# All last output transfers through SP, and a new order of the whole kernel

## The chip, the cores and the metric

One core of a Trainium2 chip (trn2). The metric is the time of one execution on the device in microseconds (us), as the median of several runs; less is better. The engines are TensorE (PE), VectorE (DVE), ScalarE (ACT), GpSimd (POOL) and SyncE (SP, here a queue that does nothing but issue DMA transfers).

## What is computed

```python
def _attn_ref(q, k, v):            # q, k, v: (4, 8, 576, 64) float32
    # 1: means over 4 neighbouring positions, full softmax attention, each row repeated 4 times
    out_up = np.repeat(sm_attn(q_d, k_d, v_d), 4, axis=2)
    # 2: softmax attention on the full sequence, |i - j| < 4 only
    out_local = np.matmul(attn, v)
    return out_up + out_local

x = attn_out.transpose(0, 2, 1, 3).reshape(B * S, H * D)   # 2304 x 512
h = (x @ w1) * (x @ w2) @ w3                               # d_ff 1024
x = h @ w_out
h = np.maximum(np.maximum(x @ w1, x @ w2), x @ w3)         # second layer, d_ff 768
out = h @ w_out                                            # 2304 x 512
```

## The kernel before, in words

The sequence of each of the 4 batches is cut into slabs. `down` (L503) does the attention on the means for one batch and one pair of heads: it loads `qk` and four `vp` planes (the first through SP, the other three through POOL, which adds them up, L515). `slab` (L604) does the attention on the band for one slab: it loads the rows of v (tile `vw`, printed as `area`) through SP in many small transfers (L629 by way of `dma`, L424); PE makes the scores (`sq`, L643); DVE and ACT the softmax (L651 to L663); PE turns it (`ptq`, L669) and multiplies by v (`poq`, L688); DVE adds the part on the means (`x32`, L697), and ACT and DVE split the sum into a high and a low part (`xt`, L449 and L451). All large products are made of three matmuls of such parts (`mm3`, L456 to L458).

Weights arrive as 64-bit words (`raw`, through SP) and are made float32 by one ACT and four DVE instructions (`float32`, L476 to L482, tiles `wf` and `cv`). While the attention of the first slabs runs, PE also makes the product of w3 and w_out (`weights_product`, `pw`, L750). When three slabs are there and the first weights, the products of the first layer begin (`front`, `pf`, L456 to L458, and `back`, `py`), and behind them those of the second (`pb`). From the first `pf` to the last `pb` the matmuls of the two layers follow one another.

Results are copied by ACT (L996) or DVE (L998) into output tiles by `put` (L985 to L1009). The tokens are done in groups `rd`; `NR - 1` is the last. Of four output rows of a group two go out singly through `dma` (L424, 128x384, 192 KB) and two as a pair (L1003, 128x2x384, 384 KB). In the last group the pairs are issued by POOL, everywhere else by SP.

The order of the work is a table: `ORDER` (L69) holds for each engine the numbers of its tasks, 2567 in all, one after another. `Program.order` merges the five lists into one program with a model of the time (`AFTER`, `RATE`, `COME`, L251 to L257); where a tile may take one of several places, the merge also says which. An engine's own instructions follow its list. SP's transfers use eight semaphores in turn, so a transfer's issue waits for the landing of the one eight ahead of it (`DMAHW0` to `DMAHW7` in the orders below).

Of the kernel before, what the change touches and what calls it, by code (L numbers as in the profile page):

```python
# [16 lines left out]
P = 128  # L17
# [117 lines left out]
    "ACT":  # L135
# [52 lines left out]
}  # L188
LAG = 1

SHORT = 2.2

WARM = 8
EARLY = 5
MM = 0.175


def view(ap, offset, dims):

# [48 lines left out]
class Program:  # L248


    AFTER = {"PE": 0.16, "DVE": 0.12, "ACT": 0.15, "POOL": 0.15, "SP": 2.3}  # L251
    RATE = 0.33e6
    ADDS, MORE = 2.2, 4.5

# [1086 lines left out]
```

## Time and profile before

| | us |
|---|---|
| median of 3 runs | 756.31 (755.21 to 756.64) |
| the profiled execution, its own time | 753.49 |
| its span in the trace | 751.7 |
| PE busy | 728.7 |
| DVE, ACT, POOL busy | 508.4, 338.7, 52.8 |
| TensorE clock, mean share of full speed | 0.990 |

The profiled execution is 2.82 us below the median of the runs, and 1.79 us above its span. PE is busy for 97% of the span, so a look at the rest, some 23 us, and at where PE ran at a low clock, tells what there is to win without less work for PE. Waits of the other engines count only where PE, or the end, waits for them.

### The profile page before, as it was taken

The page shows a single profiled execution, that of the slowest core. Times are in us where ns is not written, and L with a number is a line of the kernel's source. Part 1 is how long each engine was busy: PE and PEld are TensorE (multiplying, and loading weights), DVE is VectorE, ACT ScalarE, POOL GpSimd, SP SyncE. Part 2 cuts the span into 40 slices and gives each one's busy share as a digit, 9 for nine tenths or more (in the row PEclk, how much of TensorE's full clock was granted, in tenths as well). Part 3 has the DMA queues.
Part 4 walks back from the last instruction along what each step waited for, and adds up shares of the span by engine and source line. Part 5 has one row for each costly group of instructions (what it writes and reads, how often), then busy time and mean ns, then how long its engine had stood idle before and what let it go on. Part 6 is the DMA issues. An engine that isn't in the chain of part 4 may idle for free.

```text
span 751.7 us, 16174 instructions
## 1 busy us (share of the span) xinstructions
PE 728.7 (97%) x6636; PEld 580.8 (77%) x6636; DVE 508.4 (68%) x866; ACT 338.7 (45%) x737; POOL 52.8 (7%) x117
## 2 busy tenths in 40 slices
PE   7898999999999999999999999999999999999994
PEld 3444467777777778777888899888888888889994
DVE  6996899767334452444385789888766775488883
ACT  6672577546643673322343365532222221134683
POOL 2400401003010210000000000000000000000001
PEclk9998999999999999999999999999999999999997
DMA  9889755124332322021485696678675666786306
GB/s 335 254 246 267 180 185 143 46 66 88 94 68 66 71 65 67 14 52 36 140 308 195 211 310 227 236 276 274 220 274 196 241 241 231 276 287 225 99 30 223
DMA packets 63337, 132.72 MB, mean 177 GB/s; under 512 B 23360, under 2 KB 42608, under 8 KB 60192
## 3 DMA queue, kind: packets, MB, share of 16 engines
q1 hardware_dynamic: 58320, 126.97, 50.3%
q0 software_dynamic: 4944, 4.72, 3.8%
q8 instruction: 52, 0.85, 0.5%
q14 instruction: 21, 0.17, 0.1%
HBM read 90.28 MB, written 41.39 MB: 175 GB/s over the span
## 4 chain that ended last, share of the span: by engine, by line
PE 90%; DVE 5%; DMA 2%; issue 1%; ACT 0%; POOL 0%; POOLq 0%; SPq 0%; ACTq 0%; DVEq 0%
PE pb L456 12%; PE pb L458 12%; PE pb L457 12%; PE pf L456 9%; PE pf L458 9%; PE pf L457 9%; PE py L456 5%; PE pw L750 5%; PE py L457 4%; PE py L458 4%; PE poq L688 3%; PE sq L643 2%; PE po L589 1%; PE sp L540 1%; DVE wf L480 1%; DVE wf L482 1%
## 5 line engine op out<-in xcount | busy, mean ns | idle before, releaser
L456 PE MATMUL pf<-xt,w 128*128 128x504 f32 (+1 forms) x320 | 121.1, 378 | 0.5 <-DVE x L697 0.5
L456 PE MATMUL pb<-xc,wu 128*128 128x504 f32 (+1 forms) x324 | 120.6, 372 | 0.3
L458 PE MATMUL pb<-xc,wu 128*128 128x504 f32 (+1 forms) x324 | 119.6, 369 | 0.0
L457 PE MATMUL pb<-xc,wu 128*128 128x504 f32 (+1 forms) x324 | 119.6, 369 | 0.0
L458 PE MATMUL pf<-xt,w 128*128 128x504 f32 (+1 forms) x320 | 118.9, 372 | 0.0
L457 PE MATMUL pf<-xt,w 128*128 128x504 f32 (+1 forms) x320 | 118.7, 371 | 0.0
L456 PEld LDWEIGHTS pb<-xc,wu 128*128 128x128 f32 x324 | 60.9, 188 | 13.9 <-DVE t L912 4.1
L456 PEld LDWEIGHTS pf<-xt,w 128*128 128x128 f32 x320 | 60.1, 188 | 12.0 <-ACT dp L582 1.0
L458 PEld LDWEIGHTS pb<-xc,wu 128*128 128x128 f32 x324 | 60.9, 188 | 10.3
L914 ACT COPY t<-pb 128x504 f32<-128x504 f32 x36 | 20.9, 581 | 106.3 <-PE pb L458 93.9
L457 PEld LDWEIGHTS pb<-xc,wu 128*128 128x128 f32 x324 | 60.9, 188 | 9.8
L458 PEld LDWEIGHTS pf<-xt,w 128*128 128x128 f32 x320 | 60.1, 188 | 10.2
L457 PEld LDWEIGHTS pf<-xt,w 128*128 128x128 f32 x320 | 60.3, 188 | 9.7
L912 DVE TENSOR_TENSOR t<-t,pb 128x504 f32<-128x504 f32 x60 | 40.2, 677 | 38.2 <-PE pb L458 21.7
L750 PE MATMUL pw<-wf 128*128 128x512 f32 x128 | 61.3, 624 | 4.8 <-DVE wf L482 4.8
L456 PE MATMUL py<-g,wp 128*128 128x504 f32 (+1 forms) x160 | 63.2, 395 | 0.0
L457 PE MATMUL py<-g,wp 128*128 128x504 f32 (+1 forms) x160 | 59.6, 372 | 0.0
L458 PE MATMUL py<-g,wp 128*128 128x504 f32 (+1 forms) x160 | 59.3, 371 | 0.0
L782 DVE TENSOR_TENSOR z<-pf,z 128x504 f32<-128x504 f32 (+1 forms) x40 | 25.4, 635 | 42.6 <-PE pf L458 39.6
L750 PEld LDWEIGHTS pw<-wf 128*128 128x128 f32 x128 | 24.0, 197 | 32.2 <-issue 25.5
L458 PE MATMUL pb<-go,wm 128*128 128x252 f32 x168 | 46.8, 279 | 0.0
L456 PE MATMUL pb<-go,wm 128*128 128x252 f32 x168 | 46.8, 279 | 0.0
(140 smaller groups left out, 1339.4 us busy)
## 6 DMA issues: line engine op xcount, KB each, us to landing
wu<-w_dram SPq DMA_DIRECT2D x18, 1024.0 KB
w_dram<-hl SPq DMA_DIRECT2D x20, 512.0 KB
qk<-qkp SPq DMA_DIRECT2D x16, 576.0 KB
raw<-m SPq DMA_DIRECT2D x18, 512.0 KB
raw<-w3t SPq DMA_DIRECT2D x16, 512.0 KB
raw<-w SPq DMA_DIRECT2D x16, 512.0 KB
w_dram<-hls SPq DMA_DIRECT2D x16, 512.0 KB
m_dram<-hls SPq DMA_DIRECT2D x12, 512.0 KB
```

Source lines behind the costliest of these rows:

```text
L456: nc.tensor.matmul(o, wlo, xhi, start=first, stop=False, skip_group_check=again)
L457: nc.tensor.matmul(o, whi, xlo, start=False, stop=False, skip_group_check=again)
L458: nc.tensor.matmul(o, whi, xhi, start=False, stop=last, skip_group_check=again)
L480: prog.add(dve(n), lambda e: e.scalar_tensor_tensor(u(), high(), 0xC0000000, u(), op0=ALU.bitwise_and, op1=ALU.bitwise_or), [words], cv)
L482: prog.add(dve(n), lambda e: e.scalar_tensor_tensor(u(), low(), 29, u(), op0=ALU.logical_shift_right, op1=ALU.bitwise_or), [words], cv)
L540: e.matmul(sps[a]()[:KH, half * GD:(half + 1) * GD], s()[h, half * KH:(half + 1) * KH], s()[h, GD:2 * GD], start=True, stop=True,)
L643: e.matmul(sps[a]()[j * 32:(j + 1) * 32, (half * HP + hp) * BK:(half * HP + hp + 1) * BK], q[h, t:t + 32], k[h, t:t + BK], start=True, sto ...
L688: e.matmul(pos[hp]()[a * D:(a + 1) * D, i * BQ:(i + 1) * BQ], vw()[h, a, i], pt().rearrange("p a n -> p (a n)")[h, c:c + BQ], start=True, ...
L750: e.matmul(os[i](), w()[:, i * P:(i + 1) * P], o(), start=n == 0, stop=n == NF - 1)
L782: prog.add(psum(n), lambda e, pp=pp: e.tensor_tensor(z()[:, :n], pp()[:, :n], z()[:, :n], op=ALU.mult), [pp], [z])
L912: prog.add(dve(N), lambda e: e.tensor_tensor(ap(o), ap(x), ap(y), op=op), [x, y], [o])
L914: copy = lambda o, x: prog.add(act(N), lambda e: e.copy(ap(o), ap(x)), [x], [o])
```

## The change

```diff
+ROWS = 1.35
-    AFTER = {"PE": 0.16, "DVE": 0.12, "ACT": 0.15, "POOL": 0.15, "SP": 2.3}
-    RATE = 0.33e6
+    AFTER = {"PE": 0.16, "DVE": 0.12, "ACT": 0.15, "POOL": 0.15, "SP": 2.1}
+    RATE = 0.345e6
-    HAND, COME = 165, 45
+    HAND, COME = 165, 55
...
-                        [], [(vw, (hp, part, offset))], BV // 2 * (4096 if h == slice(0, 2) else 2048 * 7))
+                        [], [(vw, (hp, part, offset))], BV // 2 * (4096 if h == slice(0, 2) else 2048 * 7) * ROWS)
...
-                prog.add(("POOL", 1.0) if rd == NR - 1 else ("SP", 0.43), lambda e, rd=rd, j=j, o=o[0][0]: e.dma_start(
-                    out[rd * NJ + j, KX // 2:].rearrange("l p t -> p l t"), view(o(), 0, [[T, 2], [1, T]])),
-                    [t for t, _ in o], [], size=P * T * 8)
+                dma(lambda rd=rd, j=j: out[rd * NJ + j, KX // 2:].rearrange("l p t -> p l t"),
+                    lambda o=o[0][0]: view(o(), 0, [[T, 2], [1, T]]), [t for t, _ in o], [], P * T * 8)
...
-    "0 1 20 2 3 4 5 315 6 29 7 31 47 316 124 317 33 318 125 58 56 74 319 320 60 83 85 101 321 135 87 322 159 112 "
-    "110 160 114 331 137 332 138 170 194 333 195 334 172 335 173 336 447 205 337 207 338 208 458 456 474 609 611 "
+    "0 1 20 2 3 4 5 6 7 31 29 47 315 316 124 317 318 33 58 56 319 74 320 125 321 60 83 85 101 87 322 135 159 112 "
+    "160 331 110 114 332 137 138 333 170 194 334 195 335 172 336 173 337 447 205 338 207 208 458 456 474 609 611 "
```

The number 1.35 and the three rates are in the model alone: the bytes that are moved and the work that is done stay. The three pairs of the last group go through SP instead of POOL. All five lists of `ORDER` are new; of PE's the first two rows are shown (the second half of PE's list is the same as before). In them 315 to 322 and 331 to 338 are the sixteen steps of the weight product (eight matmuls each on the chip), 137 and 138 the two halves of slab 0's product with v, 205 the turn of the third slab's softmax, 609 the first product of the first layer.

On SP, around the last rows of v for slab 0 (`area<-v0`), before:

```order
L424 DMA raw_569<-w3t 128x1024 [waits DMAHW5_49]
L424 DMA raw_518<-w3t 128x1024 [waits DMAHW6_49]
L424 DMA raw_569<-w3t 128x1024 [waits DMAHW7_49]
L424 DMA area_372<-v0 15x2x512 [waits DMAHW0_49]
L424 DMA area_372<-v0 15x2x512 [waits DMAHW1_49]
L424 DMA area_372<-v0 15x2x512 [waits DMAHW2_49]
L424 DMA raw_619<-w12 128x1024 [waits DMAHW3_49,DVE_49,PE_49]
L424 DMA area_372<-v0 15x2x512 [waits DMAHW4_49]
L424 DMA area_372<-v0 15x2x512 [waits DMAHW5_49]
L424 DMA area_372<-vl 15x8x64 [waits DMAHW6_49]
```

and now (the last `v0` row here is slab 1's, the four others are slab 0's):

```order
L426 DMA area_395<-v0 15x2x512 [waits DMAHW6_49]
L426 DMA raw_447<-w3t 128x1024 [waits DMAHW7_49]
L426 DMA raw_682<-w12 128x1024 [waits DMAHW0_49,DVE_49,Activation_49]
L426 DMA area_395<-v0 15x2x512 [waits DMAHW1_49]
L426 DMA area_395<-v0 15x2x512 [waits DMAHW2_49]
L426 DMA area_395<-v0 15x2x512 [waits DMAHW3_49]
L517 DMA area_171<-vp 72x256 [waits DMAHW4_49,DMASW7_49,PE_49]
L426 DMA area_395<-v0 15x2x512 [waits DMAHW5_49]
L426 DMA raw_682<-w12 128x1024 [waits DMAHW6_49]
```

Five rows of slab 0 stood around the first `w12` load before, behind three `w3t` loads. Now the last three of slab 0 stand behind a `w12` load that waits for DVE to have converted what its buffer held, and the rows of slab 1 begin behind a `vp` load that waits for PE.

On DVE, around the additions behind slab 0's `poq`, before:

```order
L663 TENSOR_TENSOR s_684<-s_684,mx_707 128x512 [waits DVE_49]
L697 TENSOR_TENSOR x32_801<-poq_716,od_389 128x192 [waits PE_49]
L697 TENSOR_TENSOR x32_803<-poq_713,od_389 128x192
L697 TENSOR_TENSOR x32_801<-poq_719,od_389 128x192 [waits PE_49]
L477 TENSOR_SCALAR wf_520<-wf_520 128x1024
L478 TENSOR_SCALAR wf_520<-wf_520 128x1024 [waits DVE_49]
L480 SCALAR_TENSOR_TENSOR wf_520<-raw_569,wf_520 128x1024 [waits DMAHW7_49,DMAHW5_49,DVE_49]
L482 SCALAR_TENSOR_TENSOR wf_520<-raw_569,wf_520 128x1024 [waits DVE_49]
L697 TENSOR_TENSOR x32_803<-poq_710,od_389 128x192
```

and now:

```order
L665 TENSOR_TENSOR s_657<-s_657,mx_684 128x512 [waits DVE_49]
L479 TENSOR_SCALAR wf_653<-wf_653 128x1024
L480 TENSOR_SCALAR wf_653<-wf_653 128x1024 [waits DVE_49]
L482 SCALAR_TENSOR_TENSOR wf_653<-raw_447,wf_653 128x1024 [waits DMAHW7_49,DMAHW4_49,DVE_49]
L699 TENSOR_TENSOR x32_800<-poq_721,od_376 128x192 [waits PE_49]
L699 TENSOR_TENSOR x32_800<-poq_724,od_376 128x192 [waits PE_49]
L699 TENSOR_TENSOR x32_803<-poq_718,od_376 128x192
L484 SCALAR_TENSOR_TENSOR wf_653<-raw_447,wf_653 128x1024 [waits DVE_49]
L699 TENSOR_TENSOR x32_803<-poq_715,od_376 128x192
L479 TENSOR_SCALAR cv_792<-cv_792 128x1024 [waits Activation_49]
```

Three of the four conversion instructions of the last `w3t` part now stand ahead of the first addition that waits for PE. Up to the last `xt` that the first `pf` needs, DVE's list holds three conversions of `cv` (L477 to L482) where it held two; of the rest it holds as many as before.

On SP at the end, now, the nine transfers of the last group (before, the three `128x2x384` of them stood on POOL, as its last three transfers, and the six others on SP):

```order
L426 DMA out<-area_7248 128x2x384 [waits DMAHW1_49,DVE_49,Activation_49]
L426 DMA out<-area_7372 128x384 [waits DMAHW2_49,Activation_49]
L426 DMA out<-area_7372 128x384 [waits DMAHW3_49,DVE_49]
L426 DMA out<-area_7418 128x384 [waits DMAHW4_49]
L426 DMA out<-area_7320 128x2x384 [waits DMAHW5_49,DVE_49,Activation_49]
L426 DMA out<-area_7418 128x384 [waits DMAHW6_49]
L426 DMA out<-area_7701 128x384 [waits DMAHW7_49]
L426 DMA out<-area_7701 128x384 [waits DMAHW0_49,Activation_49]
L426 DMA out<-area_7248 128x2x384 [waits DMAHW1_49,Activation_49]
```

The last pair now waits for the landing of the first one, which is eight ahead of it.

## Rows read from the trace of the kernel before

**Rows 1.** The page: busy time of PE, its share of the span, instructions.
```profile
PE 728.7 (97%) x6636; PEld 580.8 (77%) x6636; DVE 508.4 (68%) x866; ACT 338.7 (45%) x737; POOL 52.8 (7%) x117
```

**Rows 2.** Stretches: window, length, busy of each engine, granted clock, DMA share, GB/s.
```profile
66.00:68.00 2.00, 2.00 (x35) 1.24 (x26) 1.30 (x4) 0.56 (x1) 0.00 (x0) 0.50 0.85 272
...
104.00:740.00 636.00, 635.16 (x5587) 534.02 (x5587) 420.24 (x712) 274.38 (x598) 24.62 (x52) 1.00 0.51 167
740.00:752.00 12.00, 0.77 (x7) 0.57 (x5) 1.33 (x7) 1.88 (x9) 2.24 (x3) 0.66 0.54 197
```

**Rows 3.** Waits of PE: for what, us in total, times, longest.
```profile
PE poq L688 <- DMA area<-v: 2.9, 1, 2.9
```

**Rows 4.** Timeline of PE: start, length, instruction, in brackets the idle time before it.
```profile
65.22 1.30 PE L688 MATMUL poq<-pt,area 30*64 30x24 f32 x60 [2.94 <-DMA area<-v]
66.45 6.12 PE L750 MATMUL pw<-wf 128*128 128x512 f32 x8
72.51 0.85 PE L688 MATMUL poq<-pt,area 30*64 30x24 f32 x64
...
75.09 3.70 PE L750 MATMUL pw<-wf 128*128 128x512 f32 x8
...
103.77 0.50 PE L456 MATMUL pf<-xt,w 128*128 128x504 f32 x1
```

**Rows 5.** Timeline of SP: its last issues of slab 0's rows of v.
```profile
56.21 2.01 SPq L424 DMA_DIRECT2D area<-v  x2
```

**Rows 6.** The chain that ended last, 52 to 66 us: start, length, what.
```profile
57.89 7.20 DMA area<-v
```

**Rows 7.** Timeline of DVE, 58 to 105 us, in brackets the idle time before.
```profile
59.03 1.22 DVE L482 SCALAR_TENSOR_TENSOR wf<-raw,wf 128x1024 uint32<-128x1024 uint32 x1
...
67.81 0.69 DVE L663 TENSOR_TENSOR s<-s,mx 128x512 f32<-128x512 f32 x1
73.41 0.89 DVE L697 TENSOR_TENSOR x<-poq,od 128x192 f32<-128x192 f32 x3 [4.91 <-PE poq L688]
...
83.10 0.69 DVE L660 TENSOR_REDUCE mx<-s 128x16 f32<-128x512 f32 x1 [0.70 <-ACT s L659]
101.84 1.15 DVE L697 TENSOR_TENSOR x<-poq,od 128x192 f32<-128x192 f32 x4 [1.27 <-PE poq L688]
```

**Rows 8.** Groups of instructions, DVE's conversion: busy us, mean ns of one, idle before.
```profile
L482 DVE SCALAR_TENSOR_TENSOR cv<-raw,cv 128x1024 uint32<-128x1024 uint32 x20 | 24.4, 1220 | 0.3
...
L478 DVE TENSOR_SCALAR cv<-cv 128x1024 uint32<-128x1024 uint32 x20 | 13.9, 696 | 0.5
L477 DVE TENSOR_SCALAR cv<-cv 128x1024 f32<-128x1024 f32 x20 | 13.9, 693 | 12.8 <-ACT cv L476 12.8
```

**Rows 9.** Stretches of 2 us at the end, columns as in rows 2.
```profile
742.00:744.00 2.00, 0.00 (x0) 0.00 (x0) 0.86 (x5) 1.04 (x5) 0.86 (x2) 0.95 0.98 354
...
748.00:750.00 2.00, 0.00 (x0) 0.00 (x0) 0.00 (x0) 0.00 (x0) 0.00 (x0) 0.50 0.15 52
```

**Rows 10.** Timeline of POOL from 735 us on.
```profile
740.35 0.79 POOL L1003 DMA_DIRECT2D out<-area  x1 [455.98 <-ACT area L996]
743.14 1.46 POOL L1003 DMA_DIRECT2D out<-area  x2 [2.00 <-DVE area L998]
```

**Rows 11.** Instructions of L1335, the program's end: ns min/median/max, first and last start.
```profile
L1335 POOLq DRAIN  x3: 46/93/7290, 743.7 to 751.4; - x3
L1335 SPq DRAIN  x3: 7/7/7, 749.2 to 751.2; - x3
```

**Rows 12.** Waits of SP from 700 us on: for what, us in total, times, longest.
```profile
SPq L1335 <- PEq L1335: 2.4, 2, 1.9
```

**Rows 13.** Output transfers, issues as in rows 11; last line: POOL's, until landed.
```profile
L424 SPq DMA_DIRECT2D out<-area x12: 332/419/580, 722.9 to 744.0; - x12
...
L1003 POOL DMA_DIRECT2D out<-area x3: 717/742/787, 740.3 to 743.9; - x3
...
DMA to landing us min/median/max: 3.0/3.9/4.9
```

196 rows, old and new, of the table ORDER are left out of this document.

## The prediction, made before the changed kernel ran

> **What bounds the kernel now.** I read the page's first part, then the stretches, then PE's waits, then the timelines of the two places where PE loses time. PE is busy for 728.7 of 751.7 us [rows 1]. From 104 to 740 us it is busy for 635.16 of 636 at full clock [rows 2]: an order can win nothing there, it can only lose. What can be won lies before 104 and after 740.
>
> Before 104 the longest wait is the one for slab 0's rows of v, 2.9 us [rows 3]. PE stands for 2.94 us before `poq`, and then runs at the low one of its two clock levels (0.50, that is 1.2 GHz, in the stretch from 66 us on [rows 2]): eight matmuls of `pw` take 6.12 us, the same eight 3.70 a little later, and sixty of `poq` 1.30 where sixty-four take 0.85 [rows 4]. So the wait costs PE 2.94 + 2.42 + 0.5 = 5.9 us. The last rows of v were issued at 56.2 to 58.2 us [rows 5], and 7.20 us passed until PE could go on [rows 6]. DVE stands for the `poq` too, 4.91 us after its work on the softmax [rows 7]. That matters because the first `pf`, at 103.77 us [rows 4], waits for DVE's additions and splits of the third slab. DVE, not PE, is the engine with least to spare until then, so its time and not PE's 5.9 us is the measure.
>
> After 740 PE works for 0.77 us more [rows 2]; the last output is copied and sent until 748 to 749 us (354 GB/s in 742 to 744, 52 GB/s in 748 to 750 [rows 9]). SP is through with its transfers at 749.2, where its first DRAIN stands [rows 11]. But POOL issues its last two pairs from 743.14 on [rows 10], and its DRAIN lasts 7.29 us, from 743.7 to 751.0 [rows 11]. SP waits 1.9 us for other engines in this last part [rows 12].
>
> **The change part by part.** The model's numbers cost nothing by themselves: no byte and no instruction follows from them, only the order, and the choice of places in the merge.
>
> *The tail.* Three issues leave POOL (0.742 us each) and come to SP (0.419 each [rows 13]), 1.26 us more on SP. SP issued the last of its six at 744.0 [rows 13]; the transfers ran until past 748, so the issues have some 4 us of cover, and the first pair, which POOL began to issue at 740.35 [rows 10], can now begin about half a microsecond sooner, since SP takes 0.419 us for what took POOL 0.742. The last pair also waits for the landing of the first; issued at 740 and landed within 3.0 to 4.9 us, as POOL's were [rows 13], it is out by 745, still inside that cover. So the bytes end where they did. What goes is POOL's wait: with no transfer of its own to drain I take the length of the other two, 0.05 to 0.09 us [rows 11]. The end then follows SP's 749.2 instead of POOL's 751.0: **-1.75 us** (751.0 - 749.2, less 0.05). Bounds: 0 if the drain does not hang on POOL's transfers, and 1.26 later if the three issues show after all; on the good side -2.25 with the half microsecond.
>
> The Trainium skill (DMA: Bandwidth & Descriptors, Issuing engines are not separate DMA queues) says that all issuers share the same 16 DMA engines, and that a second issuer saves no more than the time to initiate, small beside the transfer. By that rule alone the tail gains nothing and pays at most its issues; the trace agrees as far as the 354 GB/s go, but shows the end waiting for the issuer and not for the bytes. I go by the trace.
>
> *Slab 0's rows of v.* The last three stand behind a `w12` load that waits for a conversion on DVE. Its last instruction ran at 59.03 for 1.22 us [rows 7] and comes at much the same point in DVE's new list; so the three are issued at 61 to 62.5 us, 4 us later than before. With 7.20 us again [rows 6] PE could go on at 69.5; but SP has stood still for some microseconds ahead of them and just one weight load is in front; the shortest landing of an output pair, 3.0 us [rows 13], is the other end (65.5), and I take that one, as the nearer case. PE comes to `poq` later as well: one `pw` step (3.70 us) now lies ahead of it, so at 65.22 - 2.94 + 3.70 = 66.0. **PE's wait is about 0**, with 3.5 us as the far end.
>
> *DVE up to the first `pf`.* The wait of 4.91 us goes: three conversion instructions (0.69 + 0.70 + 1.22 = 2.61 us [rows 8]) now stand ahead of the addition, so DVE comes to it at 68.5 + 2.6 = 71.1 [rows 7], and both halves of `poq` are done by 66.0 + 2 x 0.85 = 67.7, or by 71.5 at the far end. The 0.70 us for the exponential of slab 1 [rows 7] are covered by a conversion that now stands between. Against that, one more whole conversion lies ahead of the first `pf`: 0.69 + 0.70 + 1.22 + 1.22 = 3.83 us [rows 8] (L480 does the same kind of operation on the same tile as L482, so I count it as long). Sum: 3.83 - 4.91 - 0.70 = -1.78. The conversions are also nearer behind their loads than they were; I take half a microsecond for waits on those, an estimate without a row: **-1.3 us**, `pf` at 102.5. Bounds: -3.05 if the 1.27 us that DVE waited at 101.84 [rows 7] go as well (4.91 + 0.70 + 1.27 - 3.83); +0.5 if the far end of the v rows holds and PE sets the pace (3.5 + 2.42 + 0.5 = 6.4 us on PE against 5.9 before).
>
> *From 104 to 740.* PE's work is the same and in its second half in the same order; some loads (rows of v, weights) have moved later on SP, behind transfers that wait for PE or DVE. Where PE has no wait now, each of these can only add. The least is 0, the most for one such wait what rows 4 show, 5.9 us with the clock. I take **+0.4**, near the low end, since 0.84 us in all was lost there before.
>
> Sum: -1.75 - 1.3 + 0.4 = -2.65 us. On the profiled execution's 753.49 that is 750.8; its own time stands 2.82 below the median of the runs, and I carry that offset: 756.31 - 2.65 = **753.7 us**.
>
> **The rivals.** *Nothing from the drain*: POOL's 7.29 us is something at the program's end that comes anyhow, and the two short ones are other steps of it. For it: the drain outlasts the last bytes by over 2 us, and SP, whose transfers end with them, is free sooner. Against: it starts right behind POOL's last issue. Then the tail gives 0 and the whole -0.9: 755.4.
>
> *More than the sum at the start*: DVE also loses the 1.27 us, no new waits come: -1.75 - 3.05 = -4.8, 751.5. For it: PE then reaches the last `poq` sooner; against: nearly all must go well.
>
> *v rows late again*: their far end, and PE sets the pace, `pf` at 104.3: -1.75 + 0.5 + 0.4 = -0.85, 755.5. For it: the 7.20 us of last time; against: fewer loads are in front.
>
> *A load that is too late for PE* (this one ends slower). Slab 1's rows of v, for example, stand behind a `vp` load that itself waits for PE, and SP issues strictly in turn, so all behind it wait as well. If one such load arrives 3 us after PE wants it, past the point where the clock falls, it costs what the old wait cost, 5.9 us, in a part where PE has nothing to give: 753.3 + 5.9 = 759.2. A shorter one without the clock, 1 to 3 us, ends at 754.5 to 756. For it: the new order counts SP's transfers as faster than the old one did. Against: rows of v are counted longer.
>
> The change does what it says in the lists: the three pairs stand on SP, and SP's and DVE's rows have moved; that it has no effect is not a case of its own.
>
> **How the numbers follow.** Forecast 0.47 (752.3 to 755); more at the start 0.10 (751 to 752.3); no gain from the drain 0.15 (754.8 to 756.3); v rows late 0.11 (754.8 to 757); a load too late 0.17, of which 0.05 at 754.5 to 757 and 0.12 above. A measurement of this kernel can tell about 0.2%, 1.5 us: faster is below 754.8, slower above 757.8. Faster: 0.44 of the forecast, the 0.10, 0.02 of the drain, 0.01: 0.57. Slower: 0.13. Same: 0.30. The range from 751.0 to 757.6 leaves out the slow case's upper part and the best of the start, under 2 in 10.
>
> **What would show it.** Tail: POOL's DRAIN in tenths of a microsecond, SP's wait of 1.9 us gone, last instruction some 0.8 us behind SP's first DRAIN; nine issues on SP that end before 745.5. A POOL DRAIN of several us without transfers proves the first rival. Start: PE's wait for `area<-v` under 1 us, clock 1.00 from 60 to 104, DVE's wait for the first `poq` gone, first `pf` at 102 to 103. Middle: under 1.5 us of PE's time not busy from the first `pf` on. I am wrong if PE's waits name a load (`area<-v`, `raw`, `wu`) with over 2 us, or if the clock falls again.

## The result and the profile after

| | before | after |
|---|---|---|
| median, us | 756.02 (755.21 to 756.64, 4 runs) | 748.24 (746.94 to 749.32, 4 runs) |
| the profiled execution, its own time | 753.49 | 746.94 |
| span | 751.7 | 745.2 |
| first `pf` | 103.77 | 99.78 |
| first `pf` to the end of the last matmul | 637.00 | 635.76 |
| last matmul to the end of the span | 10.95 | 9.63 |

The ratio is 0.9897, 95% interval 0.9875 to 0.9919: 7.8 us faster. The same two kernels were compared twice more, with 0.9909 (0.9891 to 0.9927) and 0.9929 (0.9905 to 0.9953). Forecast were 753.7 and a range from 751.0 to 757.6; the sign was right, the size was not.

The last three lines of the table divide the span into three stretches without a rest. They come from views of stretches; columns: window, length, busy of PE, PEld, DVE, ACT, POOL, granted clock, DMA share, GB/s. The kernel before:

```profile
60.00:103.77 43.77, 39.78 (x606) 20.32 (x604) 34.28 (x62) 20.76 (x39) 9.86 (x20) 0.92 0.65 173
103.77:740.77 637.00, 636.16 (x5592) 534.82 (x5592) 420.47 (x713) 274.61 (x598) 25.04 (x53) 1.00 0.51 166
740.77:751.72 10.95, 0.00 (x0) 0.00 (x0) 1.33 (x7) 1.88 (x9) 1.82 (x3) 0.64 0.60 216
```

The changed kernel:

```profile
60.00:99.78 39.78, 36.51 (x613) 19.39 (x611) 37.82 (x67) 20.48 (x40) 3.96 (x6) 1.00 0.68 188
99.78:735.54 635.76, 635.09 (x5592) 533.64 (x5592) 416.79 (x709) 275.13 (x598) 29.13 (x66) 1.00 0.51 165
735.54:745.17 9.63, 0.01 (x1) 0.00 (x0) 1.39 (x7) 1.90 (x9) 0.00 (x0) 0.69 0.67 242
```

Of the 6.55 us between the two profiled executions 3.99 lie before the first `pf`, 1.24 between the first `pf` and the last matmul, 1.32 behind it. In the first stretch DVE works 37.82 us instead of 34.28 (the conversion more), and yet stands idle for 2.0 us instead of 9.5. PE's clock is 1.00 instead of 0.92. In the second stretch the same 5592 matmuls are busy for 1.07 us less, at the same clock.

The start. PE's waits in the changed kernel, which answer to [rows 3]:

```profile
PE pp L581 <- ACT e L572: 2.0, 1, 2.0
PE pp L581 <- DVE x L699: 1.5, 1, 1.5
...
PE poq L690 <- DMA area<-v: 0.7, 1, 0.7
```

and its timeline of PE, which answers to [rows 4]:

```profile
66.26 1.90 PE L690 MATMUL poq<-pt,area 30*64 30x24 f32 x124 [0.66 <-DMA area<-v]
68.09 3.70 PE L752 MATMUL pw<-wf 128*128 128x512 f32 x8
...
98.07 0.67 PE L581 MATMUL pp<-ident,e 72*72 72x72 f32 x8 [1.50 <-DVE x L699]
...
99.78 0.50 PE L458 MATMUL pf<-xt,w 128*128 128x504 f32 x1 [0.30 <-ACT dp L584]
```

The wait for the rows of v is down from 2.94 to 0.66 us, and the eight `pw` behind it take 3.70 us, not 6.12. Then PE waits twice for DVE and ACT, 1.80 us together, directly ahead of the first `pf`: here DVE sets the pace, as forecast. (The wait of 2.0 us for ACT in the list above lies at 12 to 14 us; the clock is 0.62 from 16 to 20 us behind it. The kernel before has neither.) SP issued the three rows of v behind the weight load, about when the forecast said (timeline of SP):

```profile
61.42 0.33 SPq L426 DMA_DIRECT2D raw<-w  x1
61.79 1.33 SPq L426 DMA_DIRECT2D area<-v  x3
```

DVE came to the first addition at 71.3 us, and did not wait for it (timeline of DVE; no bracket, so no idle time):

```profile
70.17 1.23 DVE L482 SCALAR_TENSOR_TENSOR wf<-raw,wf 128x1024 uint32<-128x1024 uint32 x1
71.32 0.88 DVE L699 TENSOR_TENSOR x<-poq,od 128x192 f32<-128x192 f32 x3
```

The middle. PE's counted idle time in this stretch, 0.84 us before and 0.67 now, does not account for the 1.24 us. Most of it is inside blocks of `poq`. All of `poq` in this stretch (groups of instructions, first before, then now: busy us, mean ns of one, idle before):

```profile
L688 PE MATMUL poq<-pt,area 30*64 30x24 f32 x1152 | 16.8, 217 | 0.1
```

```profile
L690 PE MATMUL poq<-pt,area 30*64 30x24 f32 x1152 | 15.2, 218 | 0.0
```

That is 1.6 us less for the same matmuls; other groups take 0.1 to 0.2 us more here and there. One and the same block (the last slab's first half) in the timeline of PE of the kernel before, and then of the changed one:

```profile
357.10 1.48 PE L688 MATMUL poq<-pt,area 30*64 30x24 f32 x64
```

```profile
353.02 0.85 PE L690 MATMUL poq<-pt,area 30*64 30x24 f32 x64
```

In the kernel before six of the eighteen blocks behind the first `pf` take more than their 0.78 us from the block's start to that of the next (0.90, 0.91, 0.92, 1.15, 1.41 and 1.49 us, 2.1 us too much together, of which 0.48 in the last is counted as a wait of the `pf` behind it); in the changed kernel all eighteen take 0.77 or 0.78. The gaps between the small matmuls of such a block stand in the trace as busy time. What these matmuls wait for, no view names.

The end. Instructions of the program's end (nanoseconds min/median/max, first and last start), which answer to [rows 11], and SP's waits, which answer to [rows 12], in the changed kernel:

```profile
L1336 POOLq DRAIN  x3: 46/93/5618, 287.3 to 744.9; - x3
L1336 SPq DRAIN  x3: 7/7/7, 744.4 to 744.7; - x3
```

```profile
SPq L1336 <- DMA out<-area: 2.4, 2, 1.4
SPq L1336 <- PEq L1336: 0.7, 2, 0.5
```

POOL's DRAIN still lasts 5.6 us, but it now starts at 287.3, with POOL's last `vp` load, and is long over. SP's wait for the others is 0.5 us at the longest instead of 1.9, and the span ends 0.8 us behind SP's first DRAIN.

### The profile page after: what moved, and what is told of

Its sections match the earlier page's. It is cut to its first block, busy times and chain, and to the rows that moved or that the text cites. A ratio compares the mean times of both kernels' runs of the same rounds, so it can differ in the third digit from the quotient of the medians.

```text
span 745.2 us, 16197 instructions
## 1 busy us (share of the span) xinstructions
PE 725.9 (97%) x6636; PEld 579.0 (78%) x6636; DVE 507.9 (68%) x866; ACT 338.1 (45%) x737; POOL 48.8 (7%) x114
## 4 chain that ended last, share of the span: by engine, by line
PE 85%; DVE 10%; DMA 2%; ACT 1%; issue 1%; SPq 0%; ACTq 0%
PE pb L458 12%; PE pb L459 12%; PE pb L460 12%; PE pf L458 9%; PE pf L460 9%; PE pf L459 8%; PE py L458 5%; PE py L459 4%; PE py L460 4%; PE poq L690 2%; DVE wf L482 2%; DVE wf L484 2%; PE sq L645 2%; PE pw L752 1%; DVE wf L480 1%; DVE wf L479 1%
## 5 line engine op out<-in xcount | busy, mean ns | idle before, releaser
L752 PE MATMUL pw<-wf 128*128 128x512 f32 x128 | 59.5, 611 | 1.1 <-DVE wf L484 1.1
L784 DVE TENSOR_TENSOR z<-pf,z 128x504 f32<-128x504 f32 (+1 forms) x40 | 25.4, 634 | 34.3 <-PE pf L460 27.9
L458 PE MATMUL pb<-go,wm 128*128 128x252 f32 x168 | 46.9, 279 | 0.0
L460 PE MATMUL pb<-go,wm 128*128 128x252 f32 x168 | 46.8, 279 | 0.0
L459 PE MATMUL pb<-go,wm 128*128 128x252 f32 x168 | 46.8, 279 | 0.0
```

The costliest lines, as they stand in the source:

```text
L458: nc.tensor.matmul(o, wlo, xhi, start=first, stop=False, skip_group_check=again)
L459: nc.tensor.matmul(o, whi, xlo, start=False, stop=False, skip_group_check=again)
L460: nc.tensor.matmul(o, whi, xhi, start=False, stop=last, skip_group_check=again)
L752: e.matmul(os[i](), w()[:, i * P:(i + 1) * P], o(), start=n == 0, stop=n == NF - 1)
L784: prog.add(psum(n), lambda e, pp=pp: e.tensor_tensor(z()[:, :n], pp()[:, :n], z()[:, :n], op=ALU.mult), [pp], [z])
```

## The experiments

Each was timed beside the kernel before. Its own median varied from 753.7 to 756.0 us over these comparisons, so ratios are given. The profiles are single executions; where they fall in different clock levels, the stretches say so.

**The tail alone.** SP's list and the line in `put`, the rest as before:

```diff
-    ... 2490 2489 2556 2554 2566 2562 2552 2564
+    ... 2490 2489 2544 2556 2554 2566 2562 2552 2542 2564 2546
```

> The kernel before with one thing changed: the three pairs of the last group are issued by SP, in the places where the change has them; all else of the order as before. Theory (the end waits for POOL's DRAIN, which hangs on POOL's own transfers; SP's nine issues in a row give some 0.4 us of it back): POOL's DRAIN of 7.3 us is gone, the time from the last matmul to the end of the span falls from 10.9 to about 9.6 us, the whole is 1.3 us faster (754.7 against 756.0). Rival (the drain is there anyhow, the tail of the change is shorter by its order of copies): no gain, within 0.3 us of before, DRAIN still several us behind the last transfer.

Measured: 751.82 us (749.67 to 754.37, 12 runs) against 754.55, ratio 0.9971 (0.9954 to 0.9987). Its DRAIN and its last stretch:

```profile
L1335 POOLq DRAIN  x3: 46/93/5990, 283.8 to 749.8; - x3
...
741.22:750.03 8.81, 0.00 (x0) 0.00 (x0) 1.33 (x7) 1.88 (x9) 0.00 (x0) 0.68 0.73 264
```

The DRAIN goes where POOL's last transfer goes, so it hangs on that; the rival is out. The end is 2.14 us nearer to the last matmul (8.81 against 10.95), more than the changed kernel's 1.32. SP's first DRAIN came 7.99 us behind the last matmul (8.40 before), so the last bytes were a little earlier as well.

**The new start alone, and the new rest alone.** The first keeps the changed lists up to 99.7 us and those of before behind it, the second the lists of before up to 103.7 us and the changed ones behind it; pairs on POOL in both.

```diff
-    "0 1 20 2 3 4 5 315 6 29 7 31 47 316 ... 458 456 474 609 611 615 617 460 483 ..."
+    "0 1 20 2 3 4 5 6 7 31 29 47 315 316 ... 458 456 474 609 611 615 617 460 483 ..."
```

```diff
-    "... 458 456 474 609 611 615 617 460 483 485 621 ..."
+    "... 458 456 474 609 611 615 617 621 460 622 623 ..."
```

> The kernel before in all but the start: the tasks that the changed kernel begins in its first 99.7 us, in the changed order; behind them everything in the order of before, pairs on POOL. Theory (the start alone brings 4.0 us, since the rest of PE's work is fixed): first pf at 99.8 us and the span 4.0 shorter, 752.0; with the clock falling in some executions at the wait for slab 0's rows of v, up to 2.3 more in those. Rival (the start is earlier, but what it left undone is paid behind it, as stalls on late loads and conversions): first pf at 99.8, gain under 2 us, with new waits of PE between 100 and 200 us.

> The reverse of the run before: the first 103.7 us in the order of before, all behind it in the changed order, pairs on POOL. Theory (between the first pf and the last matmul the change saves 1.2 us, by waits inside poq blocks that the trace does not count as idle): first pf at 103.8, first pf to last matmul 635.8 against 637.0, whole 754.8 against 756.0; the poq blocks behind the start all take 0.78 us, while five of before take 0.9 to 1.5. Rival (the 1.2 us came from the earlier start, as work that was moved ahead of the first pf): first pf to last matmul 637 as before, no gain.

Measured: the new start 752.51 us, 0.9967 (0.9951 to 0.9984), some 2.5 us faster, where 4.0 were expected. In its profile the rows of v were late (timeline of PE), the clock fell at 69 us, and once more ahead of the first `pf` (stretch):

```profile
67.33 0.30 PE L689 MATMUL poq<-pt,area 30*64 30x24 f32 x4 [1.65 <-DMA area<-v]
...
99.97 1.06 PE L580 MATMUL pp<-ident,e 72*72 72x72 f32 x8 [1.35 <-DVE x L698]
```

```profile
100.00:102.00 2.00, 2.00 (x16) 1.56 (x16) 1.35 (x5) 1.35 (x4) 0.00 (x0) 0.52 1.07 365
```

So the first `pf` was at 102.13 here. The rival's new waits between 100 and 200 us are not there; what is missing is the clock. The new rest went slower, 759.28 us, 1.006 (1.004 to 1.0081). That is no verdict on the changed order: the cut mixes two lists just where the first products begin, and PE stood there (timeline of PE):

```profile
108.16 0.49 PE L457 MATMUL pf<-xt,w 128*128 128x504 f32 x1 [3.70 <-ACT dp L583]
```

The chain of its trace runs there from a weight load (`raw<-w`, until 102.9) through DVE's conversion (`cv`, until 105.4) and ACT's split of `w` and copies (until 108.1) to that `pf`. As far as this chain shows, the new rest wants the weight earlier than the old start has it ready. The other half of the expectation held: none of the `poq` blocks behind the start is long. Its last stretch has the changed order of copies with the pairs still on POOL:

```profile
741.84:753.46 11.62, 0.00 (x0) 0.00 (x0) 1.38 (x7) 1.89 (x9) 1.82 (x3) 0.58 0.57 203
```

**The changed kernel again,** twice, beside others.

> The changed kernel itself, beside the three below on the same chip. Theory (its runs differ by whether the clock falls at a wait of 1 to 3 us ahead of slab 0's poq or ahead of the first pf, since PE's work is fixed): its times scatter over 2 to 3 us between 746.5 and 749.5, the profiled execution shows the low clock level in stretches before 110 us only, and the ratio to before is 0.990 to 0.992. Rival (one constant time, scatter of the measurement): the profile's clock is the same as in the first trace and the times within 1 us.

> The changed kernel itself beside it, as the measure for the run above. Theory: 0.990 of before, 747 to 749, with the low clock level in stretches before 110 us in some executions.

Measured: 747.77 (746.57 to 749.85, 6 runs) and 748.25 (747.02 to 750.83, 7 runs), the ratios given above. The profiled executions are slower than the first trace, and in both the clock fell behind 60 us. The first of them, timeline of PE and two stretches:

```profile
66.71 1.81 PE L690 MATMUL poq<-pt,area 30*64 30x24 f32 x124 [1.05 <-DMA area<-v]
...
99.15 0.67 PE L581 MATMUL pp<-ident,e 72*72 72x72 f32 x8 [1.36 <-DVE x L699]
```

```profile
70.00:72.00 2.00, 2.00 (x3) 0.67 (x2) 1.97 (x4) 1.14 (x1) 0.00 (x0) 0.50 0.71 214
...
100.00:104.00 4.00, 4.00 (x17) 3.05 (x15) 3.15 (x7) 4.00 (x10) 1.22 (x4) 0.58 0.97 344
```

Two stretches at the low level, first `pf` at 100.93. In the other one it was at 102.12. So the first trace, with 99.78 and a full clock from 60 us on, is a good execution of the changed kernel, while that of before is an ordinary one with the clock fallen.

**Slab 0's rows of v ahead of the weight load, in the changed kernel.** SP's list:

```diff
-    ... 123 309 347 119 118 121 436 ...
+    ... 123 309 119 118 121 347 436 ...
```

> The changed kernel with slab 0's last three rows of v issued by SP ahead of the w12 load that waits for DVE, instead of behind it. Theory (DVE sets the first pf, the rows of v only decide over PE's wait and the clock): PE's wait for area<-v is gone, first pf at 99.0 to 99.8 as before the edit, median 0 to 1.5 us below the changed kernel, with fewer executions at the slow end. Rival (the rows of v still bound the start): first pf 0.7 or more earlier in the profile, median 2 us lower or more. Another rival (the w12 load, now later, is late for DVE): first pf later by 0.5 to 2 us.

Measured: 748.05 us, 0.9915 (0.99 to 0.9929), the same as the changed kernel beside it (0.9909). PE's wait for these rows was gone and the clock 1.00 from 60 to 96 us, but PE waited for DVE instead, and the first `pf` was at 101.57, later than the theory's 99.8. The last rival's number came, its cause did not: no load is among DVE's waits up to there. In the changed kernel these three rows no longer bind.

**The old order of the tail, in the changed kernel.** SP's list, and DVE's and ACT's lists of copies with it:

```diff
-    ... 2544 2556 2566 2552 2542 2562 2554 2564 2546
+    ... 2544 2556 2554 2566 2562 2552 2542 2564 2546
```

> The changed kernel with the order of copies and output transfers of the last 20 us taken from the kernel before (nine transfers, all on SP, as in the run with the tail alone). Theory (the tail's gain is the absent DRAIN alone, 1.8 us or more, and the new order of the copies gives back 0.8 of it, since SP's issues come late): last matmul to end of the span 8.8 us, against 9.6 in the changed kernel, whole 0.8 us faster. Rival (both orders end with the same transfers): 9.6 us, no gain.

Measured: 747.98 us, 0.9914 (0.9899 to 0.9928). Last stretch:

```profile
737.15:745.79 8.64, 0.00 (x0) 0.00 (x0) 1.32 (x7) 1.87 (x9) 0.00 (x0) 0.73 0.74 270
```

In the trace the theory holds: 8.64 us behind the last matmul, 1.0 less than the change's 9.63. SP's last issue ends 4.80 us behind the last matmul, with the changed order 5.84. The medians do not resolve that 1 us, but all fifteen traces of this case agree on it: with the old order of copies the stretch is 10.8 to 11.0 us with the pairs on POOL (four traces) and 8.6 to 8.8 on SP (five), with the changed order 11.6 on POOL (one) and 9.6 to 9.7 on SP (five). So the move to SP is worth some 2 us with either order, and the new order of the copies costs 0.7 to 1.0.

**Slab 0's rows of v earlier, in the kernel before.** One edit, SP's list:

```diff
-    ... 147 153 463 308 295 309 116 121 120 381 122 119 151 ...
+    ... 147 153 116 121 120 122 119 463 308 295 309 381 151 ...
```

> The kernel before with only one thing changed: slab 0's last five rows of v are issued ahead of the vp load at 52 us and of the three weight loads behind it, so at 48 to 51 us instead of 54 to 58. Theory (the start's gain is that wait: 2.94 us of PE, the clock behind it and the 4.91 us in which DVE stood; no other part of the new order is needed for it): PE's wait for area<-v is gone, the clock stays at 1.00 from 60 to 80 us, first pf at 98.5 to 100, whole 4 us faster than before. Rival (DVE's new order is needed as well, since DVE was the engine with least to spare): first pf at 102 or later, gain under 2 us. Another rival (the weight loads, now later, stop DVE and PE): pw waits for wf L482 by 2 us more.

Measured: 750.82 us (750.41 to 752.63, 6 runs), ratio 0.9953 (0.9939 to 0.9967), 3.5 us faster. Timeline of SP, timeline of PE, and the stretch up to the first `pf`:

```profile
48.21 2.36 SPq L425 DMA_DIRECT2D area<-v  x5
```

```profile
64.15 3.70 PE L751 MATMUL pw<-wf 128*128 128x512 f32 x8
```

```profile
60.00:100.89 40.89, 37.16 (x607) 19.00 (x605) 34.32 (x62) 21.55 (x39) 8.54 (x20) 1.00 0.73 186
```

No wait for `area<-v`, no low clock, first `pf` at 100.89, with DVE's list as it was: DVE's 34.3 us of work fit, with 6.6 us idle instead of 9.5. Five transfers issued 6 to 8 us sooner bring no less than the whole new start did in its own run (0.9953 against 0.9967), and DVE's new order is not needed for it: the first rival is out. So is the second: PE's waits for conversions ahead of `pw` are 4.6 us in all, 4.8 before. The theory was 0.9 us too good for the first `pf`; PE now waits for DVE ahead of `poq` and `ptq`, 1.06 and 1.43 us.

**One conversion later, in the changed kernel.** DVE's and ACT's lists:

```diff
-    ... 454 386 472 473 216 215 210 209 212 218 476 ...
+    ... 454 472 473 216 215 210 209 212 218 386 476 ...
...
-    ... 455 389 211 217 459 387 ...
+    ... 455 211 217 459 389 387 ...
```

> The changed kernel with one conversion instruction of DVE (the last of the third cv part, 1.2 us, and ACT's copy that reads it) moved from ahead of the third slab's additions to behind its splits, so that the first pf does not wait for it. Theory (in the changed kernel DVE alone sets the first pf, and the 1.4 to 1.6 us that PE waits ahead of it bring the clock down in some executions): PE's wait for x before pp falls below 0.8 us, the clock stays at 1.00 from 96 to 110 us, first pf 0.7 to 1.0 us earlier where all else is equal, median 1 to 2.5 us below the changed kernel's 747.8. Rival (PE, by the last poq, sets it as well): the wait falls but first pf does not move, gain under 0.5 us plus the clock. Another rival: the conversion is now late for the fourth pf task, and PE waits there instead.

Measured: 749.44 us, 0.9928 (0.991 to 0.9946): nothing won. The second rival came, one product sooner than it said (timeline of PE, stretch):

```profile
98.74 0.67 PE L582 MATMUL pp<-ident,e 72*72 72x72 f32 x8 [0.59 <-DVE x L700]
...
105.42 0.50 PE L459 MATMUL pf<-xt,w 128*128 128x504 f32 x1 [1.96 <-ACT dp L585]
```

```profile
104.00:110.00 6.00, 4.58 (x13) 3.70 (x14) 5.31 (x7) 5.44 (x16) 1.08 (x5) 0.72 1.07 328
```

The wait ahead of the first `pf` fell from 1.50 to 0.59 us, and came back behind its twelve matmuls as 1.96 us, with the clock.

**The new middle alone.** The changed lists from 200 to 396 us of the kernel, all else as before:

```diff
-    "... 1246 1248 1299 1252 1301 1253 1254 1302 ... 1346 1315 1348 1316 1317 1349 1318 1358 ..."
+    "... 1246 1299 1248 1252 1253 1301 1254 1302 ... 1346 1315 1316 1348 1317 1349 1318 1358 ..."
```

> The kernel before with the changed order only for what the changed kernel does from 200 us of the kernel before up to 396 us; start and end as before, pairs on POOL. Theory (the middle's gain comes from waits inside poq blocks that are not counted as idle): the blocks after 200 us all take 0.78 us (before, four of them take 0.9 to 1.4), first pf to last matmul 636 instead of 637.0, whole 1.0 us faster than before. Rival (the middle's gain came out of the start, not out of its own order): first pf to last matmul 637, no gain, though the blocks are short.

Measured: 753.58 us, 0.9976 (0.9954 to 0.9997). The stretch from the first `pf` to the last matmul:

```profile
105.12:740.81 635.69, 634.80 (x5592) 533.58 (x5592) 420.62 (x713) 274.23 (x598) 24.75 (x53) 1.00 0.51 167
```

635.69 us where the kernel before has 637.00, with no long block of `poq` behind 200 us. The order alone wins 1.3 us where PE was busy for over 99%. The other traces with the clock at 1.00 behind the first `pf` say the same: 636.96 and 637.06 with the old middle (the tail alone; the rows of v earlier, in the kernel before), 635.76 and 635.71 with the new one (the changed kernel; the three parts below).

**Towards something better.** The moved conversion with the old tail, and these two with the rows of v ahead of the weight load.

> The changed kernel with the moved conversion and the old order of the tail together. Theory: the two gains add, some 1 us of the tail and 1 to 2 of the start, 745.5 to 746.5 where the changed kernel has 747.8. Rival: the tail's 1 us alone, 747.

> The same as the run of both edits, and slab 0's last three rows of v ahead of the w12 load. Theory (with DVE no longer the bound, PE's wait for the rows and the clock behind it count): 0.5 to 1.5 us below the run of both edits, clock 1.00 from 60 to 80 us. Rival (still DVE): the same as the run of both edits, within 0.5 us.

Measured: 749.34 us, 0.9919 (0.9899 to 0.9939), and 748.43 us, 0.9912 (0.9893 to 0.9931). Neither beats the changed kernel (0.9897 to 0.9929 in its three comparisons). In their traces the tail gives its 1 us (8.7 us behind the last matmul), and the moved conversion costs it and more (639.1 and 637.9 us from the first `pf` to the last matmul, against 635.76).

**Three parts alone.** The kernel before with the edit to the rows of v, the new middle and the tail on SP.

> The kernel before with three parts alone: slab 0's last five rows of v earlier on SP, the changed order from 200 to 396 us, the three last pairs on SP in the old tail. DVE's order of the start stays that of before, with one conversion fewer ahead of the first pf. Theory (these three make up the change's whole gain, each in its own place, and DVE's new order at the start adds nothing that lasts): the ratios multiply, 0.9953 x 0.9971 x 0.9976 = 0.990, the changed kernel's own 0.990; first pf at about 100.9, from there to the last matmul 635.7, from there to the end 8.8, a span of 745.4. Rival (DVE's new order carries part of the gain): slower than the changed kernel by 1 us or more. Another rival (the old tail and fewer falls of the clock are worth more than DVE's order): 0.5 to 1.5 us faster than the changed kernel.

Measured: 749.43 us (747.76 to 750.16, 8 runs), 0.9939 (0.9916 to 0.9962), beside the changed kernel's 748.25 and 0.9929: the intervals lie over one another. Its stretches:

```profile
103.06:738.77 635.71, 634.84 (x5592) 533.64 (x5592) 420.31 (x713) 274.41 (x598) 24.32 (x52) 1.00 0.51 167
738.77:747.55 8.78, 0.00 (x0) 0.00 (x0) 1.33 (x7) 1.87 (x9) 0.00 (x0) 0.71 0.74 265
```

Middle and tail came out as worked out (635.7 and 8.8). The start did not: in this execution PE waited longer for conversions of weights, and the first `pf` was at 103.06 (PE's waits):

```profile
PE pw L751 <- DVE wf L483: 6.5, 3, 4.0
```

The wait of 4.0 us ends at 14.66, far ahead of the edit, where the order is that of the kernel before (which waits 2.12 us there), and the clock fell behind it. So this trace does not tell what the three parts do to the start. The medians are 1.2 us apart, as the first rival had it, but within the noise: whether DVE's new start is worth that stays open.

The three parts of the change alone (tail, new start, new middle) multiply to 0.9971 x 0.9967 x 0.9976 = 0.991, where the whole change has 0.990 to 0.993: nothing large is left over.

## Why the prediction was wrong

The measured 748.2 is 5.4 us below the forecast. By the sum's terms, 2.7 us of that lie at the start, 1.6 from 104 to 740 us, 1.5 in the offset, and the tail takes back 0.4.

**The tail, -1.75.** The mechanism was right: SP is free at 744.4, no DRAIN of POOL holds up the end, the nine issues end before the bytes do. The term was 1.32 in the change and 2.14 with the tail alone. What the step left out is that the order of the copies changed as well: the changed one lets SP end its issues 1.0 us later than the old order does, so the bytes end later (SP's first DRAIN 8.81 us behind the last matmul, 8.40 before). That the bytes would end where they did was not true of this order. The first rival is out by the DRAIN at 283.8 and 287.3; the prediction's sign for it, a DRAIN of several us without output transfers, was badly chosen, since one of 5.6 us is still there and costs nothing. By the Trainium skill's sentence on issuers (DMA: Bandwidth & Descriptors, Issuing engines are not separate DMA queues) the tail would have gained nothing; 2.14 us were measured, and the measurement decides.

**The rows of v.** Issue times were nearly right (61.8 to 63.1 us for 61 to 62.5), and PE's wait was 0.66 us in the first trace. "About 0" was too good for the other two: PE stood there for 1.05 us in one and 1.81 in the other (1.65 of it put down to DVE), and behind it the clock fell, which the prediction had named as a sign of being wrong. (Its far end for both halves of `poq`, 71.5, should be 69.5 + 2 x 0.85 = 71.2; nothing rests on it.)

**DVE up to the first `pf`, -1.3.** This is the step whose size failed most. It counted two of DVE's waits as won (4.91 + 0.70) and took half a microsecond back. But DVE's idle time between 60 us and the first `pf` fell from 9.5 to 2.0 us, by 7.5, against 3.5 us of added work: -3.99. The bound of -3.05 was made from single rows too and did not hold for these two executions. The sum should have been made over the whole stretch: 9.5 us of idle time in it, less the added work, were the most that an order could win. Part of the 3.99 is that the two executions differ in clock. In the profiles where it had fallen behind slab 0's wait, the old start (before, the tail alone, the new middle) gave 103.77, 104.26 and 105.12, the new one (the changed kernel twice, the old tail order, the new start alone) 100.93, 102.12, 101.15 and 102.13: 104.4 against 101.6 on average, 2.8 us. Where it had not, 101.46 (the new rest) against 99.78, 1.7 us. Both are more than the term and inside its bounds; the rest of the 3.99 goes with the clock, which fell in one of the two executions and not in the other, and for which the sum had no term.

**From 104 to 740, +0.4.** "An order can win nothing there, it can only lose" was wrong, and with it the sign of the term. It read busy time as work. The long blocks of `poq` held 2.1 us, they are gone, and 1.24 us remain of that over the stretch. The new middle alone gave 1.3. No load was late there, so the slow rival did not come.

**The offset.** 2.82 us between the profiled execution and the median were carried over (2.53 with the fourth run of before); in the changed kernel it is 1.30. That is the rest of the 7.8 us; with the clock falling in some executions and not in others, one profile tells a median to some 2 us only. The gain itself is not luck with the clock. At a mean clock of 0.994 the changed kernel took 746.9 us (median of 5 executions) and the one before 752.5 (of 7), at 0.987 and 0.988 749.3 (of 5) and 756.0 (of 21), over all comparisons.

## What to carry to other kernels

Before a stretch at 99% busy is called full, measure the same block of work in several places: a block that takes twice as long as its neighbours holds a wait, even if the trace counts none. For what an order can win, sum the idle time of the engine that sets the pace over the whole stretch, not the two or three longest waits. And look at whose queue the program's end waits for: in the kernel before the end waited until 751.0 for POOL's DRAIN of 7.29 us, though no byte moved after 749.

## What was not expected of the hardware

POOL's long DRAIN began with the issue of POOL's last transfer in all fifteen traces. It lasted 5.4 to 6.3 us where that was a `vp` load at 284 to 292 us, and 6.7 to 7.3 where it was an output pair at the end; it costs only where the end waits for it.

The length of PE's wait alone did not tell whether the clock fell. After 2.94 us ahead of `poq` in the kernel before it fell; after 2.77 us at the same place in the run of the new rest it stayed at full level. After 1.50 us ahead of `pp` in the changed kernel it stayed, after 1.36 us in the next execution of that kernel it fell; ahead of `poq` in the run with the old tail it fell after 0.90 us. The stretch behind the wait of 2.77 us, with the clock in the third column from the right:

```profile
68.00:70.00 2.00, 2.00 (x6) 0.73 (x4) 0.77 (x2) 0.00 (x0) 0.47 (x1) 1.00 0.72 241
```

Single executions of one kernel differ by 2 us and more here, and go with the clock: the changed kernel's seventeen took 746.6 to 747.4 us at a mean clock of 0.994 (five of them), and 750.8 at 0.984 (one).
